# First weight chunks on a second DMA queue, values behind the first queries, first sums turned in one group, denominators ahead of the values' turning

## The chip, the cores and the metric

The kernel runs on one core of one Trainium2 chip. The metric is the device time of one execution in microseconds. A profiled execution also gives a span, from the program's first instruction to its last; it is some 1.7 us shorter than the time. Engines are named as in the profile: PE (TensorE matmul), PEld (TensorE weight load), DVE (VectorE), ACT (ScalarE), POOL (GpSimd), SP (SyncE, which issues most of the transfers).

A ratio below is the mean time of one kernel's fast runs over the mean of the other's fast runs of the same rounds, so it is not quite the ratio of the medians that stand beside it.

## The reference

An attention with sketched polynomial features, then a SwiGLU block:

```python
a = einsum('rd,bhsd->bhsr', S1, x); b = einsum('rd,bhsd->bhsr', S2, x)   # x: q or k, r = 8
phi(x) = outer product of a and b, 64 features
kv  = einsum('bhsf,bhsd->bhfd', phi(k), v);  z = sum over s of phi(k)
att = (phi(q) @ kv) / (phi(q) @ z + 1e-6)          # 4 batches, 4 heads, 1088 tokens, 32 wide
x   = att as (4352 tokens, 128)
out = (silu(x @ w_gate) * (x @ w_val)) @ w_out      # 1536 wide inside
```

Inputs arrive as 64-bit floats, which the engines don't have. Each weight chunk is therefore loaded as integers and made fp32 in steps: two on DVE, two on ACT, two on DVE, one product on POOL. The text calls this narrowing.

## The kernel before

Batch 0's attention is written out by hand, because everything waits for it: sketch, key features, sums, query features, totals, division. Its 1088 tokens are handled in three blocks. As soon as the first block of `xT` is there, the feed-forward units (`unit(i, j)`: block i, chunk j of the inner width) start, and the other batches' attention is spread among them. The parts that the change touches (cuts marked):

```python
def narrow(dst, raw, shape):            # one weight chunk, in three yields
    ...                                 # DVE 2 steps; ACT 2 steps; DVE 2 steps
    mul = nc.vector if first else nc.gpsimd
    mul.tensor_tensor(out=dst, in0=f, in1=e[:].bitcast(FP32), op=ALU.mult)
    ...
keep_warm(98, 32); keep_warm(18, 64)    # filler matmuls, so that PE's clock comes up
...                                     # sketch matmuls, keep_warm(3) of 512 columns, key products
key_values(kv, phk, *fpieces[0]); key_values(kv, phk, *fpieces[1])
phq = query_features(n, pss, qbs)
zp = bank("g2")
for h in range(H):                      # select the sums of a head's features ...
    nc.tensor.matmul(zp[32*h:32*h+32, 0:F], sel[:], zq[:, F*h:F*h+F], start=True, stop=True)
key_values(kv, phk, *fpieces[2])
nc.vector.tensor_copy(zs[:], zp[:, 0:F])
turn_q(*steps[1])
for t, s, to, tag in ((1, zs, None, "g0"), (0, kvs, kv, "g1")):   # ... and turn sums, then values
    ...
    turn_kv(s[:], ps)
    nc.scalar.copy(kvz[t][:], ps[:, 0:P])
...
nd = totals(n, phq, kvz, ...)           # denominators, then numerators
divide(0, *steps[0], nd, among=("wv", 0))
```

Of the kernel before, what the change touches and what calls it, by code (L numbers as in the profile page):

```python
# [7 lines left out]
FP32 = mybir.dt.float32  # L8
# [4 lines left out]
ALU = mybir.AluOpType  # L13
# [4 lines left out]
def kernel(  # L18
# [28 lines left out]
    nc = tc.nc  # L47
    P = nc.NUM_PARTITIONS
# [37 lines left out]
    def bank(tag=None):  # L86
        if tag is None:
            tag = free_banks[turn[0] % len(free_banks)]
            turn[0] += 1
        return psum.tile([P, TB], FP32, tag=tag, name="bank")  # L90
# [29 lines left out]
    def load_q(b, x0=0, x1=NX):  # L120
        src = q[b].rearrange("h (pp x) d -> (h pp) x d", pp=32)
        nc.sync.dma_start(out=qld[:, x0:x1, :], in_=src[:, x0:x1, :])

    def load_v(b, queues):
        src = v[b].rearrange("h (pp x) d -> pp h x d", pp=32)
        for a, queue in enumerate(queues):
            n = min(NC, NX - NC * a)
            queue.dma_start(
                out=vld[32 * a : 32 * a + 32, :, 0:n, :],
                in_=src[:, :, NC * a : NC * a + n, :],  # L130
            )
# [2 lines left out]
    coming = [(w, i) for i in range(len(pieces["wg"])) for w in ("wg", "wv")]  # L134
    coming += [("wo", i) for i in range(len(pieces["wo"]))]

    def load_next():
        if not coming:
            return
        name, i = coming.pop(0)  # L140
        dst, src = weights[name]
        c0, c1 = pieces[name][i]
        if name == "wo":
            part = src.rearrange("(c p) d -> p c d", p=P)[:, c0:c1, :]
        else:
            part = src.rearrange("p (c f) -> p c f", f=P)[:, c0:c1, :]
        if not wide_w:
            nc.sync.dma_start(out=dst[:, c0:c1, :], in_=part)
            return
        t = raw[name, i] = stage.tile([P, 3, P], I64, tag="raw", name="raw", bufs=NRAW)  # L150
        nc.sync.dma_start(out=t[:, 0 : c1 - c0, :], in_=part)

    nc.sync.dma_start(out=sraw[0:R, :], in_=S1)
    nc.scalar.dma_start(out=sraw[R : 2 * R, :], in_=S2)
# [2 lines left out]
    nc.gpsimd.memset(vld[96:128, :, NC - 2 : NC, :], 0.0)  # L157
    load_k(0)
    load_q(0, 0, 2 * XS)
    for i in range(NRAW if wide_w else len(coming)):  # L160
        if i == 2:
            load_v(0, [nc.sync] * 4)
            load_q(0, 2 * XS, 4 * XS)
        load_next()
    load_q(0, 4 * XS, NX)



# [22 lines left out]
    def keep_warm(n, w=TB, ps=None):  # L191


        if ps is None:
            ps = bank(free_banks[turn[0] % len(free_banks)])
        for _ in range(n):
            nc.tensor.matmul(  # L197
                ps[0:32, 0:w], warm[:, 0:32], warm[:, 0:w], start=True, stop=True
            )

    def narrow(dst, raw, shape):






        words = raw.bitcast(I32)
        pat = "p (n w) -> p n w" if len(shape) == 2 else "p c (n w) -> p c n w"
        words = words.rearrange(pat, w=2)  # L210
        lo = words[..., 0].bitcast(U32)
        hi = words[..., 1]
        first = len(shape) == 2
        tag = "s" if first else ""
        e, m = (
            stage.tile(shape, I32, tag=n + tag, name=n, bufs=6) for n in ("exp", "man")
        )
        f = m[:].bitcast(FP32)
        nc.vector.tensor_scalar(e[:], hi, 0x7FF00000, None, op0=ALU.bitwise_and)  # L219
        nc.vector.tensor_scalar(  # L220
            m[:], hi, 0xFFFFF, 0x100000, op0=ALU.bitwise_and, op1=ALU.bitwise_or
        )
        yield
        nc.scalar.activation(e[:], e[:], AF.Relu, bias=rebias[: shape[0], :], scale=8.0)  # L224
        nc.scalar.activation(f, m[:], AF.Copy, scale=2.0**-20)  # L225
        yield
        nc.vector.scalar_tensor_tensor(  # L227
            out=e[:], in0=hi, scalar=-(1 << 31), in1=e[:],
            op0=ALU.bitwise_and, op1=ALU.bitwise_or,
        )  # L230
        nc.vector.scalar_tensor_tensor(  # L231
            out=f, in0=lo, scalar=2.0**-52, in1=f, op0=ALU.mult, op1=ALU.add
        )
        mul = nc.vector if first else nc.gpsimd
        mul.tensor_tensor(out=dst, in0=f, in1=e[:].bitcast(FP32), op=ALU.mult)  # L235
        if not first:
            load_next()
        yield
# [8 lines left out]
    def run(*gens):  # L247
        for g in gens:
            for _ in g:
                pass  # L250
# [76 lines left out]
    def turn_kv(kvs, kzp):  # L327

        for half in range(2):
            nc.tensor.matmul(  # L330
                kzp[F * half : F * half + F, 0:P], kvs, ident[:], start=True, stop=True
            )

    def query_products(x0, n, tags):

        w = 32 * n
        pss = []
        for pr in range(2):
            if isinstance(tags[pr], str):
                both = wide(tags[pr])[:].rearrange("p g (t w) -> p g t w", t=2)  # L340
                parts = [both[:, g] for g in range(2)]
            else:
                both = None
                parts = [
                    bank(t)[:].rearrange("p (t w) -> p t w", t=2) for t in tags[pr]
                ]
            for t in range(2):
                for half in range(2):
                    for g in range(2):
                        r = slice(64 * pr + 32 * g, 64 * pr + 32 * g + 32)  # L350
                        nc.tensor.matmul(  # L351
                            parts[g][F * half : F * half + F, t, 0:w],
                            sq[r, t, :, :].rearrange("p i j -> p (i j)"),
                            qT[r, x0 : x0 + n, half, :],
                            start=True,
                            stop=True,
                        )
            pss.append((both, parts))
        return pss
# [31 lines left out]
    def halves(x):  # L391
        return x if isinstance(x, list) else [x[:, 0, :], x[:, 1, :]]

    def totals(n, phq, kvz, nd):

        w = 32 * n
        for t in (1, 0):
            for h in range(H):
                for half in range(2):
                    r = slice(F * half, F * half + F)  # L400
                    nc.tensor.matmul(  # L401
                        halves(nd[t])[half][32 * h : 32 * h + 32, 0:w],
                        kvz[t][r, 32 * h : 32 * h + 32],
                        phq[r, h, 0:w],
                        start=True,
                        stop=True,
                    )
        return nd
# [5 lines left out]
    def divide(b, x0, n, nd, among=()):  # L414
# [8 lines left out]
            out=dT[:, 0 : 2 * n, :].rearrange("p (a x) t -> p a x t", a=2),  # L423
            in_=nd[1][:, :, 0:w].rearrange("p a (x t) -> p a x t", t=32),
        )
        nc.vector.tensor_scalar_add(rc[:, 0 : 2 * n], dT[:, 0 : 2 * n, 0], 1e-6)
        nc.vector.reciprocal(rc[:, 0 : 2 * n], rc[:, 0 : 2 * n])
        nc.vector.transpose(
            out=rd[:, 0 : 2 * n, :], in_=rc[:, 0 : 2 * n].unsqueeze(2).to_broadcast([P, 2 * n, 32])
        )  # L430
        if among:
            part(*among)
        xs = xT[:, t0 : t0 + 2 * w].rearrange("p (x a t) -> p a x t", a=2, t=32)
        rs = rd[:, 0 : 2 * n, :].rearrange("p (a x) t -> p a x t", a=2)
        flat, deep = "p (x t) -> p x t", "p a (x t) -> p a x t"
# [150 lines left out]


    keep_warm(98, 32)
    keep_warm(18, 64)
    fills = {(w, i): narrow_w(w, i) for w in weights for i in range(len(pieces[w]))}  # L590

    def part(name, i):

        next(fills[name, i], None)

    s32 = sraw
    if wide_s:
        s32 = const.tile([2 * R, Dh], FP32, name="s32")
        run(narrow(s32[:], sraw[:], [2 * R, Dh]))
    srep = bank("g0")  # L600
    for h in range(H):
        nc.tensor.matmul(
# [3 lines left out]
            start=True,  # L606
            stop=True,
        )
    keep_warm(3, ps=bank("acc"))
    sTv = srep[:, 0 : 2 * R].rearrange("p (t r) -> p t r", t=2)  # L610
    nc.vector.tensor_tensor(
        out=s12[:],
# [24 lines left out]
    part("wg", 0)  # L637
    part("wv", 0)
    zq = apool.tile([P, H * F], FP32, tag="zq", name="zq")
    kvs, zs = (apool.tile([P, F], FP32, name=x) for x in ("kvs0", "zs0"))  # L640
    kvz = [apool.tile([P, P], FP32, name=x) for x in ("kvz0", "kvz1")]
    qbs.append(query_copy(n, *pss[1]))
    nc.scalar.copy(zq[:], kz)
    part("wg", 0)
    key_values(kv, phk, *fpieces[0])
    key_values(kv, phk, *fpieces[1])
    phq = query_features(n, pss, qbs)
    zp = bank("g2")
    for h in range(H):
        nc.tensor.matmul(  # L650
            zp[32 * h : 32 * h + 32, 0:F], sel[:], zq[:, F * h : F * h + F],
            start=True, stop=True,
        )
    key_values(kv, phk, *fpieces[2])
    nc.vector.tensor_copy(zs[:], zp[:, 0:F])
    turn_q(*steps[1])
    for t, s, to, tag in ((1, zs, None, "g0"), (0, kvs, kv, "g1")):
        if to is not None:
            nc.vector.tensor_copy(s[:], to)
        ps = bank(tag)  # L660
        turn_kv(s[:], ps)
        nc.scalar.copy(kvz[t][:], ps[:, 0:P])
    part("wv", 0)
    part("wg", 0)
    nd = totals(n, phq, kvz, ([bank(t) for t in ("g2", "acc")], side_by_side("a")[0]))
    pss = query_products(*steps[1], ("b", ("g0", "g1")))
    qbs = [query_copy(steps[1][1], *ps) for ps in pss]
    turn[0] = 2
    keep_warm(3, ps=wide("a")[:, 0, :])
    divide(0, *steps[0], nd, among=("wv", 0))  # L670



# [11 lines left out]
    part("wg", 2)  # L685
    part("wv", 2)
    turn_q(*steps[2])
    unit(0, 2, late=True)
    part("wg", 2)
    unit(1, 0, late=True)  # L690
    pss = query_products(*steps[2], "ab")
    qbs = [query_copy(steps[2][1], *ps) for ps in pss]
# [110 lines left out]
```

## Time and profile before

| | before |
|---|---|
| time, median of 4 executions | 322.15 us (322.0 to 322.41) |
| span of the profiled execution (its time: 321.65 us) | 319.9 us |
| PE busy | 312.2 us |
| first feed-forward unit starts | 16.06 us |
| second unit's value matmuls start | 20.44 us |

The number to follow is the last row. From there on PE has work without an end, and the rest of the program took 299.5 us, so a gain must show as an earlier start of the second unit's value matmuls. The prediction shows the lines of the page, of the stretches, of the chain of waits and of the timeline (start, us, engine, line, operation, output<-inputs, form, count). Two more lines of the kernel before's timeline (start, us, engine, line, operation, output<-inputs, form, count) matter for what follows: the group that selects the sums, and the numerators:

```profile
11.04 0.31 PE L650 MATMUL bank<-zq,sel 128*32 128x64 f32 x8
...
13.11 0.56 PE L401 MATMUL bank<-phq,kvz 64*32 64x192 f32 x16
```

`128*32` is the stationary tile (rows by columns), and the count is in instructions. The next group in PE's order started at 11.18, so the eight took 0.14 us of PE's order.

### The profile page before, as it was taken

Reading aid. Unit: us, or ns where it says so; the run is one execution under the profiler, and the core shown is the slowest. Engines: PE = TensorE matmul, PEld = TensorE weight load, DVE = VectorE, ACT = ScalarE, POOL = GpSimd, SP = SyncE. Lnnn points to the kernel's source line nnn. Section 1 sums busy time; section 2 is a strip of 40 time slices with the busy share of each in tenths; the row PEclk is TensorE's granted clock in tenths of the full one; section 3 lists DMA queues with packets and bytes.
Section 4 is the critical chain, followed back from the end, with each engine's and each line's share of the span. In section 5 each row is a group of like instructions: output and inputs, shape, how many; then the busy total and the mean of one; then the engine's idle time right before and its main releaser. Section 6 shows DMA issues by size and latency. Waiting matters only on the chain.

```text
span 319.9 us, 5604 instructions
## 1 busy us (share of the span) xinstructions
PE 312.2 (98%) x2300; PEld 193.7 (61%) x2300; DVE 157.8 (49%) x332; ACT 99.0 (31%) x227; POOL 37.6 (12%) x53
## 2 busy tenths in 40 slices
PE   8989999999999999999999999999999999999994
PEld 6545565655556665555666656555667655676664
DVE  4887999442556532554643542354544332323321
ACT  3467755321211322222322222313222222222230
POOL 2324234072000230000000060000000000000000
PEclk9999999999999999999999999999999999999999
DMA  7553490204041201100210100100010100100101
GB/s 206 155 151 100 162 243 2 72 0 97 2 94 27 65 22 50 27 0 2 39 58 0 22 2 0 24 4 2 0 27 0 21 0 2 26 0 0 21 2 25
DMA packets 24665, 13.99 MB, mean 44 GB/s; under 512 B 18368, under 2 KB 22720, under 8 KB 24640
## 3 DMA queue, kind: packets, MB, share of 16 engines
q1 hardware_dynamic: 24000, 13.54, 16.7%
q8 instruction: 18, 0.29, 0.4%
q10 hardware_dynamic: 640, 0.10, 0.2%
q14 instruction: 7, 0.06, 0.1%
HBM read 11.41 MB, written 2.23 MB: 43 GB/s over the span
## 4 chain that ended last, share of the span: by engine, by line
PE 88%; DVE 7%; issue 2%; ACT 1%; POOL 0%; DVEq 0%
PE bank L519 49%; PE bank L547 27%; DVE hj L533 2%; PE a L351 2%; PE a L401 2%; PE b L351 1%; PE bank L197 1%; PE a L307 1%; DVE exp L227 1%; PE a L561 1%; DVE man L231 1%; PE b L401 1%; PE a L276 1%; DVE exp L219 1%; ACT exp L224 1%
## 5 line engine op out<-in xcount | busy, mean ns | idle before, releaser
L533 DVE TENSOR_TENSOR hj<-sg,bank 128x384 f32<-128x384 f32 (+1 forms) x138 | 72.7, 528 | 118.2 <-PE bank L519 117.3
L525 ACT ACTIVATE sg<-bank 128x384 f32<-128x384 f32 (+1 forms) x144 | 67.9, 472 | 162.7 <-PE bank L519 161.9
L519 PE MATMUL bank<-xT,wg 128*128 128x384 f32 (+1 forms) x288 | 113.7, 477 | 1.2 <-POOL wg L235 1.1
L519 PE MATMUL bank<-xT,wv 128*128 128x384 f32 (+1 forms) x288 | 111.5, 469 | 0.5 <-DVE hj L533 0.5
L547 PE MATMUL bank<-hj,wo 128*128 128x384 f32 (+2 forms) x288 | 106.8, 462 | 0.3 <-DVE hj L533 0.2
L519 PEld LDWEIGHTS bank<-xT,wv 128*128 128x128 f32 x288 | 54.4, 190 | 34.5 <-DVE hj L533 2.1
L547 PEld LDWEIGHTS bank<-hj,wo 128*128 128x128 f32 x288 | 53.9, 190 | 33.2 <-issue 2.4
L519 PEld LDWEIGHTS bank<-xT,wg 128*128 128x128 f32 x288 | 52.7, 190 | 32.3 <-issue 3.9
L453 POOL TENSOR_TENSOR zs<-phk 128x1024 f32<-128x1024 f32 x3 | 7.0, 2348 | 115.5 <-PE bank L519 106.0
L379 DVE TENSOR_TENSOR phq<-a,qb 128x384 f32<-128x384 f32 (+1 forms) x11 | 5.8, 531 | 10.7 <-ACT qb L365 10.7
L365 ACT COPY qb<-a 128x384 f32<-128x384 f32 (+1 forms) x11 | 5.1, 460 | 15.1 <-PE b L351 8.6
L351 PE MATMUL a<-qT,sq 32*64 32x192 f32 (+1 forms) x176 | 9.2, 324 | 0.0
L351 PE MATMUL b<-qT,sq 32*64 32x192 f32 (+1 forms) x176 | 9.2, 324 | 0.0
L227 DVE SCALAR_TENSOR_TENSOR exp<-raw,exp 128x384 int32<-128x384 int32 (+2 forms) x14 | 8.6, 618 | 0.9 <-ACT exp L224 0.9
L224 ACT ACTIVATE exp<-exp,rebias 128x384 int32<-128x384 int32 (+3 forms) x15 | 8.2, 550 | 2.7 <-DVE exp L219 2.0
L422 DVE STREAM_TRANSPOSE dT<-a 128x384 f32<-128x384 f32 (+1 forms) x8 | 4.4, 550 | 7.8 <-PE a L401 7.8
L365 ACT COPY qb<-b 128x384 f32<-128x384 f32 (+1 forms) x11 | 5.1, 463 | 9.7 <-PE b L351 6.4
L575 DVE STREAM_TRANSPOSE o<-bank 128x384 f32<-128x384 f32 (+2 forms) x12 | 6.6, 549 | 2.7 <-PE bank L547 2.3
L351 PEld LDWEIGHTS a<-qT,sq 32*64 32x64 f32 x176 | 5.5, 131 | 3.9 <-issue 3.0
L379 DVE TENSOR_TENSOR phq<-b,qb 128x384 f32<-128x384 f32 (+1 forms) x11 | 5.8, 527 | 4.2 <-ACT qb L365 4.2
L231 DVE SCALAR_TENSOR_TENSOR man<-raw,man 128x384 f32<-128x384 uint32 (+2 forms) x14 | 6.9, 493 | 0.0
L225 ACT ACTIVATE man<-man 128x384 f32<-128x384 int32 (+3 forms) x15 | 6.7, 450 | 0.5 <-DVE man L220 0.5
(96 smaller groups left out, 168.9 us busy)
## 6 DMA issues: line engine op xcount, KB each, us to landing
kld<-in_k_dram SPq DMA_DIRECT2D x4, 544.0 KB, 4.1
vld<-in_v_dram SPq DMA_DIRECT2D x12, 144.0 KB, 4.3
qld<-in_q_dram SPq DMA_DIRECT2D x3, 544.0 KB, 3.9
raw<-in_moe_w_out_dram SPq DMA_DIRECT2D x4, 384.0 KB, 5.8
out_dram<-o SPq DMA_DIRECT2D x28, 48.0 KB, 1.9
raw<-in_moe_w_gate_dram SPq DMA_DIRECT2D x3, 384.0 KB, 3.3
raw<-in_moe_w_val_dram SPq DMA_DIRECT2D x3, 384.0 KB, 3.5
out_dram<-o SPq DMA_DIRECT2D x16, 40.0 KB, 1.7
```

What stands on the lines that cost most here:

```text
L224: nc.scalar.activation(e[:], e[:], AF.Relu, bias=rebias[: shape[0], :], scale=8.0)
L227: nc.vector.scalar_tensor_tensor(out=e[:], in0=hi, scalar=-(1 << 31), in1=e[:], op0=ALU.bitwise_and, op1=ALU.bitwise_or,)
L231: nc.vector.scalar_tensor_tensor(out=f, in0=lo, scalar=2.0**-52, in1=f, op0=ALU.mult, op1=ALU.add)
L351: nc.tensor.matmul(parts[g][F * half : F * half + F, t, 0:w], sq[r, t, :, :].rearrange("p i j -> p (i j)"), qT[r, x0 : x0 + n, half, :], s ...
L365: nc.scalar.copy(qb[:, :, 0:w], both[:, :, 1, 0:w])
L379: nc.vector.tensor_tensor(out=phq[:, 2 * pr : 2 * pr + 2, 0:w], in0=both[:, :, 0, 0:w], in1=qb[:, :, 0:w], op=ALU.mult,)
L401: nc.tensor.matmul(halves(nd[t])[half][32 * h : 32 * h + 32, 0:w], kvz[t][r, 32 * h : 32 * h + 32], phq[r, h, 0:w], start=True, stop=True,)
L453: add = lambda o, a, b: nc.gpsimd.tensor_tensor(out=o, in0=a, in1=b, op=ALU.add)
L519: nc.tensor.matmul(o[:, 0:n], w[:, j, :], xT[:, t0 : t0 + n], start=True, stop=True)
L525: nc.scalar.activation(sg[:, 0:n], g[:, 0:n], AF.Silu)
L533: nc.vector.tensor_tensor(out=hj[:, 0:n], in0=sg[:, 0:n], in1=u[:, 0:n], op=ALU.mult)
L547: nc.tensor.matmul(acc[i][:, 0:n], wo[:, j, :], hidden[i, j][:, 0:n], start=(j == 0), stop=(j == NCH - 1),)
```

## The change

It aims at the first 20 us. The first two weight chunks go to ACT's queue, so that SP can issue the values sooner; fewer and shorter fillers stand ahead of the sketch matmuls; the sums are turned in one group of small matmuls instead of by selecting, copying and turning; the denominators no longer wait for the values' turning; POOL's product of a two-chunk piece is cut in halves. The core of the diff:

```diff
     load_k(0)
     load_q(0, 0, 2 * XS)
-    for i in range(NRAW if wide_w else len(coming)):
-        if i == 2:
-            load_v(0, [nc.sync] * 4)
-            load_q(0, 2 * XS, 4 * XS)
-        load_next()
-    load_q(0, 4 * XS, NX)
+    load_v(0, [nc.sync] * 4)
 ...
+        p2 = e[:].bitcast(FP32)
+        for c in [slice(0, 1), slice(1, 2)] if shape[1] == 2 else [slice(None)]:
+            mul.tensor_tensor(out=dst[:, c], in0=f[:, c], in1=p2[:, c], op=ALU.mult)
 ...
+    def turn_sums(sums, weights, ps):
+        for h in range(H):
+            for half in range(2):
+                nc.tensor.matmul(
+                    ps[F * half : F * half + F, Dh * h : Dh * h + Dh],
+                    sums[:, F * h : F * h + F], weights, start=True, stop=True)
 ...
-    keep_warm(18, 64)
+    keep_warm(9, 64)
 ...
+    for _ in range(2):
+        load_next(nc.scalar)
+    load_q(0, 2 * XS, 4 * XS)
 ...
-    keep_warm(3, ps=bank("acc"))
+    keep_warm(2, ps=ps)
+    keep_warm(16, 32, ps=ps)
 ...
+    phq = query_features(n, pss, qbs, pairs=(0,))
+    turn_q(*steps[1])
+    query_features(n, pss, qbs, phq=phq, pairs=(1,))
+    ps = bank("g0")
+    turn_sums(zq, sel[:], ps)
+    nc.scalar.copy(kvz[1][:], ps[:, 0:P])
     key_values(kv, phk, *fpieces[2])
+    nc.vector.tensor_copy(kvs[:], kv)
+    totals(n, phq, kvz, nd, which=(1,))
+    turn_kv(kvs[:], ps)
 ...
+    totals(n, phq, kvz, nd, which=(0,))
 ...
+    part("wg", 2)
     unit(0, 2, late=True)
-    part("wg", 2)
```

In `divide`, the last narrowing steps of the first gate chunk now stand between the turn of the denominators and the reciprocal.

More of the change, by code (lines that the diff above doesn't have):

```diff
@@ L135, with load_next @@
     coming += [("wo", i) for i in range(len(pieces["wo"]))]
-    def load_next():
+    def load_next(queue=nc.sync):
         if not coming:
@@ L147, in load_next @@
         if not wide_w:
-            nc.sync.dma_start(out=dst[:, c0:c1, :], in_=part)
+            queue.dma_start(out=dst[:, c0:c1, :], in_=part)
             return
         t = raw[name, i] = stage.tile([P, 3, P], I64, tag="raw", name="raw", bufs=NRAW)
-        nc.sync.dma_start(out=t[:, 0 : c1 - c0, :], in_=part)
+        queue.dma_start(out=t[:, 0 : c1 - c0, :], in_=part)
     nc.sync.dma_start(out=sraw[0:R, :], in_=S1)
@@ L234, in narrow @@
         mul = nc.vector if first else nc.gpsimd
-        mul.tensor_tensor(out=dst, in0=f, in1=e[:].bitcast(FP32), op=ALU.mult)
+        p2 = e[:].bitcast(FP32)
+        for c in [slice(0, 1), slice(1, 2)] if shape[1] == 2 else [slice(None)]:
+            mul.tensor_tensor(out=dst[:, c], in0=f[:, c], in1=p2[:, c], op=ALU.mult)
         if not first:
@@ L332, in turn_kv @@
             )
+    def turn_sums(sums, weights, ps):
[3 more added lines that the diff above has]
+                    ps[F * half : F * half + F, Dh * h : Dh * h + Dh],
+                    sums[:, F * h : F * h + F],
+                    weights,
+                    start=True,
+                    stop=True,
+                )
     def query_products(x0, n, tags):
@@ L392, in halves, with totals @@
         return x if isinstance(x, list) else [x[:, 0, :], x[:, 1, :]]
-    def totals(n, phq, kvz, nd):
+    def totals(n, phq, kvz, nd, which=(1, 0)):
         w = 32 * n
-        for t in (1, 0):
+        for t in which:
             for h in range(H):
@@ L425, in divide @@
         )
+        for name in among[:1]:
+            part(name, 0)
         nc.vector.tensor_scalar_add(rc[:, 0 : 2 * n], dT[:, 0 : 2 * n, 0], 1e-6)
@@ L430, in divide @@
         )
-        if among:
-            part(*among)
+        for name in among[1:]:
+            part(name, 0)
         xs = xT[:, t0 : t0 + 2 * w].rearrange("p (x a t) -> p a x t", a=2, t=32)
@@ L596 @@
     s32 = sraw
+    steps_s = iter(())
     if wide_s:
         s32 = const.tile([2 * R, Dh], FP32, name="s32")
-        run(narrow(s32[:], sraw[:], [2 * R, Dh]))
+        steps_s = narrow(s32[:], sraw[:], [2 * R, Dh])
+        next(steps_s)
+        next(steps_s)
+    for _ in range(2):
+        load_next(nc.scalar)
+    load_q(0, 2 * XS, 4 * XS)
+    for _ in range(2, NRAW if wide_w else len(coming) + 2):
+        load_next()
+    load_q(0, 4 * XS, NX)
+    run(steps_s)
     srep = bank("g0")
@@ L608 @@
         )
-    keep_warm(3, ps=bank("acc"))
+    ps = bank("acc")
+    keep_warm(2, ps=ps)
+    keep_warm(16, 32, ps=ps)
     sTv = srep[:, 0 : 2 * R].rearrange("p (t r) -> p t r", t=2)
@@ L639 @@
     zq = apool.tile([P, H * F], FP32, tag="zq", name="zq")
-    kvs, zs = (apool.tile([P, F], FP32, name=x) for x in ("kvs0", "zs0"))
+    kvs = apool.tile([P, F], FP32, name="kvs0")
     kvz = [apool.tile([P, P], FP32, name=x) for x in ("kvz0", "kvz1")]
+    nc.scalar.copy(zq[:], kz)
     qbs.append(query_copy(n, *pss[1]))
-    nc.scalar.copy(zq[:], kz)
-    part("wg", 0)
     key_values(kv, phk, *fpieces[0])
     key_values(kv, phk, *fpieces[1])
-    phq = query_features(n, pss, qbs)
-    zp = bank("g2")
-    for h in range(H):
-        nc.tensor.matmul(
-            zp[32 * h : 32 * h + 32, 0:F], sel[:], zq[:, F * h : F * h + F],
-            start=True, stop=True,
-        )
-    key_values(kv, phk, *fpieces[2])
-    nc.vector.tensor_copy(zs[:], zp[:, 0:F])
-    turn_q(*steps[1])
-    for t, s, to, tag in ((1, zs, None, "g0"), (0, kvs, kv, "g1")):
-        if to is not None:
-            nc.vector.tensor_copy(s[:], to)
-        ps = bank(tag)
-        turn_kv(s[:], ps)
-        nc.scalar.copy(kvz[t][:], ps[:, 0:P])
+    phq = query_features(n, pss, qbs, pairs=(0,))
[4 more added lines that the diff above has]
+    nc.scalar.copy(kvz[1][:], ps[:, 0:P])
+    part("wg", 0)
+    key_values(kv, phk, *fpieces[2])
+    nc.vector.tensor_copy(kvs[:], kv)
+    nd = [bank(t) for t in ("g2", "acc")], side_by_side("a")[0]
+    totals(n, phq, kvz, nd, which=(1,))
+    ps = bank("g1")
+    turn_kv(kvs[:], ps)
+    nc.scalar.copy(kvz[0][:], ps[:, 0:P])
     part("wv", 0)
-    part("wg", 0)
-    nd = totals(n, phq, kvz, ([bank(t) for t in ("g2", "acc")], side_by_side("a")[0]))
+    totals(n, phq, kvz, nd, which=(0,))
     pss = query_products(*steps[1], ("b", ("g0", "g1")))
@@ L669 @@
     keep_warm(3, ps=wide("a")[:, 0, :])
-    divide(0, *steps[0], nd, among=("wv", 0))
+    divide(0, *steps[0], nd, among=("wg", "wv"))
     att = attention(1)
```

## The prediction

> **What bounds the kernel now.** I read the page first. TensorE (PE) is busy for 312.2 of 319.9 us, so at most 7.7 us can be won without doing less matrix work, and the change removes almost none. Then I summed busy time by stretch, to see where those 7.7 us lie.
>
> ```profile
> PE 312.2 (98%) x2300; PEld 193.7 (61%) x2300; DVE 157.8 (49%) x332; ACT 99.0 (31%) x227; POOL 37.6 (12%) x53
> ...
> 16.00:20.00 4.00, 2.85 (x37) 1.56 (x38) 3.93 (x14) 2.26 (x6) 1.53 (x2) 1.00 0.59 122
> 20.00:24.00 4.00, 4.00 (x20) 2.00 (x26) 2.99 (x9) 2.82 (x7) 0.35 (x1) 1.00 0.45 179
> ...
> 310.00:320.00 10.00, 5.78 (x37) 4.86 (x35) 1.85 (x4) 0.49 (x1) 0.00 (x0) 0.97 0.11 20
> ```
>
> The first pair of columns is a stretch and its length, the next five are busy us of PE, PEld, DVE, ACT, POOL. About 4.2 us of PE's idle time is the ending (310 on), which the change doesn't touch; PE is full from 20 us on, apart from short stops near 36 and 43 us. So the only thing to move is when the full stream starts. Before that PE looks busy, but much of it is filler (line 197, matmuls that keep its clock up) and small steps of the first head's attention. What sets the start stands in the chain of waits (start, us, what):
>
> ```profile
> 4.90 0.34 PE bank L602 x8
> ...
> 5.55 1.40 DVE kT L260 x3
> ...
> 11.43 0.23 DVE zs L655
> 11.66 0.48 DVE qT L266
> 12.14 0.12 DVE kvs L659
> ...
> 12.31 0.44 PE bank L330 x4
> 12.75 0.57 PE a L401 x16
> ...
> 13.34 0.59 DVE dT L422
> ...
> 15.38 0.53 DVE xT L447 x2
> 15.92 0.20 DVE exp L219
> ...
> 18.46 1.19 POOL wg L235
> ...
> 19.69 4.20 PE bank L519 x12
> ```
>
> From 11.4 to 18.4 us this is VectorE (DVE) nearly without a break; then GpSimd (POOL) multiplies the second gate chunk, and the full stream of line 519 starts at 19.69. The timeline gives the details there:
>
> ```profile
> 18.46 1.18 POOL L235 TENSOR_TENSOR wg<-man,exp 128x256 f32<-128x256 f32 x1 [2.55 <-DVE man L231]
> ...
> 19.60 0.74 POOL L235 TENSOR_TENSOR wv<-man,exp 128x256 f32<-128x256 f32 x1
> ...
> 20.40 0.30 PEld L519 LDWEIGHTS bank<-xT,wv 128*128 128x128 f32 x2 [0.41 <-POOL wv L235]
> ```
>
> The wait on weights ends at 20.40 with the value chunk, and from there PE paces itself (0.645 us for a 384-wide pair of fp32 matmuls).
>
> **What the Trainium skill says.** "DMA: Bandwidth & Descriptors", section "Issuing engines are not separate DMA queues", says that transfers issued by different engines run on the same 16 DMA engines and interleave; a second issuer only saves its sequencer's time. "Queues, rings and completion order" adds that each DMA engine takes turns between queues with work, a packet at a time. The trace agrees with the first: from 4 to 10 us the DMA share is 0.96 to 1.18, so the engines themselves are full, and the issue saved is two of 0.43 us on SP. "GPSIMD Engine Reference", section "Key points", says that POOL shares its SBUF interfaces with VectorE and contends with instructions of two SBUF inputs. The trace agrees: the same 128x256 product took 1.18 us beside such instructions and 0.74 us beside others; 128x128 took 0.46 and 128x384 1.00. "TensorE: Matmul & The Clock Gate", section "What's actually happening", says that PE starts at half clock and needs about 3.4 us of sustained work; no run here shows yet that fewer fillers keep it up, but the change keeps PE filled until about 5.5 us, and the first full-clock record of this trace is at 5.4 us.
>
> **The change part by part.**
>
> 1. *Loads.* The first two 128 KB weight chunks go from SP, ahead of the values, to ScalarE (ACT), whose two issues fall at 3.2 to 4.3 us, before its copies at 5.6. The values are issued about 0.95 us earlier, but the last of their four waits for the keys' landing as before (issued at 5.43, landed 4.8 us later, 10.24). The DMA engines have the same bytes to move before it: keys, two thirds of queries, two weight chunks, values. So I expect the values within 0.3 us of 10.24. Earlier would not help: the matmuls with them (10.34) stand in PE's order behind the key sums, whose last third waits for a POOL product that ends at 9.69. Later would hurt. The keys land at 5.42 and start everything; the ACT queue's weights become ready from about 4.2 us (estimate: SP's key issue at 1.28 had its first packet at 2.28, so 1.0 us after), when few key packets remain. Cost: 0 to 0.2 us, taken as 0.1.
>
> 2. *Fillers.* Nine 64-wide ones (0.062 us each, 1.12/18) go from ahead of the sketch matmuls, so these start at about 4.35 instead of 4.90, and the sketch tile is ready at about 4.8. But the key transposes behind it wait for the keys at 5.42 anyway. Gain 0 to 0.1 us: hidden by a transfer.
>
> 3. *First sums turned in one group.* Before: 4 selecting matmuls, a DVE copy (zs, 0.23), 2 turning matmuls, an ACT copy (0.27), and these behind the turn of the queries on DVE. After: 8 small matmuls straight from ACT's copy zq give the turned sums, and one ACT copy ends it. In detail: zq is ready at 10.98 as before, the value matmuls of the first two thirds hold PE until 11.04, the 16 instructions of the group at about 0.015 us (as the value matmuls, 0.70/48) until 11.28; result 0.17 us later at 11.45; ACT, now with its two query copies behind zq, is free at 11.5 and copies until 11.77. The denominators start at about 11.83 instead of 12.68. They take 0.43, so the turn dT starts at about 12.4 instead of 13.34: 0.9 us sooner.
>
> 4. *Order behind it.* On DVE the two narrowing steps of wg (0.25 + 0.28) now stand behind dT instead of before it, so half of that is given back. Adding durations from the timeline: dT to 13.0, narrowing to 13.5, sum and reciprocal to 13.93, rd to 14.5, narrowing of wv to 14.9, the two xT products to 15.45. Before: 15.92. So 0.5 us is won on DVE. The numerators hardly move: ACT does the first narrowing (0.4 + 0.3) between the two copies, so the second copy ends near 13.0 (before 13.06), and numerators, query products and fillers on PE come about 0.1 sooner. The first unit at 16.06 thus gains 0.1 only, bound by PE's own order. The query copies on ACT (to 15.7) are in time for DVE, which from xT runs through four narrowing steps (0.8), three feature products (1.05) and four more steps (1.4) without a wait: POOL can start the second gate chunk at about 18.0 instead of 18.46.
>
> 5. *Split product on POOL.* Two halves of 0.46 instead of one of 0.74: 0.18 us more in all per chunk, but the unit that waits needs only the first half. Gate halves and first value half: 3 x 0.46 = 1.38, plus up to the 0.44 of contention seen in the old 1.18: done at 19.4 to 19.8, and PE takes it 0.06 later. Before 20.40. So PE's stream starts 0.5 to 0.95 us sooner, middle 0.7.
>
> 6. *Last move*, the ACT half of wg's third chunk ahead of a unit: ACT does the same work in another order, and had 1.18 us free in 20 to 24. No cost or gain expected.
>
> Sum on the path: keys +0.1, DVE and POOL together -0.7, so -0.6; 322.25 - 0.6 = 321.65. From 28 to 51 us the chain goes through DVE, but its first link (dT at 28.24) waits 1.2 us for PE's denominators and so moves with PE. After 52 us PE runs full, and the shift is carried to the end unchanged. I place the middle at 321.6.
>
> **The rivals.** (a) *Hidden altogether*: the numerators, which hardly move, or the full DVE gives the time back, and the result is 322.1 to 322.4. For it: DVE is busy 3.93 of 4 us in 16 to 20, and part 4 removes only one 0.23 us copy from it. Against: the removed waits in 11.4 to 14 were DVE's idle time (0.8 us in 12 to 16). (b) *The loads turn worse*: the weights on the second queue get in among the keys or the values. For it: DMA engines are full. Each 0.1 us by which keys or values are late lengthens the run by nearly 0.1, as the whole chain hangs on the keys; with 0.5 us late keys 322.1, with both late perhaps 322.6. Against: the keys are nearly through by then. (c) *More than I count*: values and keys land sooner, POOL meets no contention, and the third chunk's earlier ACT steps save a DVE wait (0.94 us before its step at 23.66): 320.9. Against: that DVE wait is not on the chain, and POOL's product would have to run beside other DVE instructions.
>
> **Range and chances.** Rival (a) gives the upper part, (c) the lower; (b) lies mostly outside. Runs of before spread by 0.35 us. I say 321.6 us, 320.9 to 322.2. A 2% step is 6.4 us, nearly all the idle time that PE has, and nothing in the change costs that much: faster 0.01, same 0.98, slower 0.01.
>
> **What would show it.** In the changed profile the keys should land near 5.4 to 5.6 and the transposes start then (parts 1, 2); the first denominators' turn should start near 12.4 (part 3) and the first xT near 14.9 (part 4); the first unit's line should start near 15.95; POOL's second gate chunk near 18.0 in two pieces, and the second unit's value matmuls near 19.6 (part 5), with PE full from there. It would be wrong if the transposes start at 5.8 or later, if the value matmuls start after 10.6, or if the second unit starts 0.7 us sooner and the distance from it to the end grows.

## The result, and the profile after

| | before | after |
|---|---|---|
| time, median of 4 executions | 322.15 us (322.0 to 322.41) | 322.17 us (321.36 to 322.5) |
| span of the profiled execution | 319.9 us | 319.6 us |
| PE busy | 312.2 us | 311.5 us |
| second unit's value matmuls start | 20.44 us | 20.13 us |

The ratio is 0.9996, with a 95% interval of 0.9975 to 1.0017: the same. The median lies within the predicted range, near its upper end, and 0.57 us above the predicted 321.6. Two things call for an explanation. The profiled execution gained 0.3 us and not 0.6. And it was the quickest of the four: the others took 322.5, 322.39 and 321.95, a spread of 1.1 us where the kernel before had 0.4. The profiled execution of the kernel before was a quick one as well: it took 321.65, less than any of the four timed ones. So the two traces compare two quick executions, 321.65 with 321.36.

The page of the kernel after, and its stretch from 16 to 20 us and its ending, in the columns that the prediction explains:

```profile
PE 311.5 (97%) x2310; PEld 193.6 (61%) x2310; DVE 157.7 (49%) x331; ACT 98.9 (31%) x227; POOL 37.9 (12%) x55
```

```profile
16.00:20.00 4.00, 3.19 (x38) 1.48 (x38) 3.90 (x14) 2.26 (x6) 1.65 (x3) 1.00 0.70 177
...
310.00:320.00 10.00, 5.49 (x36) 4.59 (x34) 1.75 (x4) 0.49 (x1) 0.00 (x0) 0.89 0.11 21
```

PE's busy time in 16 to 20 grew from 2.85 to 3.19, and that in the last stretch fell from 5.78 to 5.49: the whole stream has moved forward by 0.3 us, as it is the same stream. DVE is still full, at 3.90 of 4.

The chain of waits of the kernel after:

```profile
1.28 4.04 DMA kld<-in_k_dram
...
5.35 1.50 DVE kT L257 x3
...
10.45 0.87 PE b L304 x48
11.32 0.59 PE bank L335 x16
11.91 0.47 PE b L304 x24
12.38 0.57 PE a L410 x16
...
12.97 0.58 DVE dT L431
...
15.27 0.53 DVE xT L458 x2
...
18.35 0.91 POOL wg L232
...
19.30 4.32 PE bank L530 x12
```

The chain begins with the keys' transfer, as the sketch tile no longer ends later than the keys. From 10.45 to 12.95 it is PE: the value matmuls (line 304), the new group (line 335), the rest of the value matmuls, the denominators (line 410). The new group holds 0.59 us. Then DVE carries it to 18.28, POOL's product of the second gate chunk follows, and the second unit starts at 19.30.

The timeline shows the group and three places behind it:

```profile
11.25 0.55 PEld L335 LDWEIGHTS bank<-sel,zq 128*64 128x64 f32 x16
...
13.60 0.56 PE L410 MATMUL bank<-phq,kvz 64*32 64x192 f32 x16 [0.36 <-ACT kvz L682]
...
18.35 1.32 POOL L232 TENSOR_TENSOR wg<-man,exp 128x128 f32<-128x128 f32 x2 [2.54 <-DVE man L226]
...
19.62 0.86 POOL L232 TENSOR_TENSOR wv<-man,exp 128x128 f32<-128x128 f32 x2
...
20.13 0.30 PEld L530 LDWEIGHTS bank<-xT,wv 128*128 128x128 f32 x2 [0.53 <-POOL wv L232]
```

The group's weight loads alone are busy for 0.55 us. The numerators start at 13.60, which is 0.49 later than before. POOL needs 1.32 us for the two halves of the gate chunk, 0.91 of it for the first (the chain has it), and the second unit's value matmuls wait for the value chunk's first half until 20.13.

### The profile page after: what moved, and what is told of

Its sections match the earlier page's. It is cut to its first block, busy times and chain, and to the rows that moved or that the text cites. A ratio compares the mean times of both kernels' runs of the same rounds, so it can differ in the third digit from the quotient of the medians.

```text
span 319.6 us, 5629 instructions
## 1 busy us (share of the span) xinstructions
PE 311.5 (97%) x2310; PEld 193.6 (61%) x2310; DVE 157.7 (49%) x331; ACT 98.9 (31%) x227; POOL 37.9 (12%) x55
## 4 chain that ended last, share of the span: by engine, by line
PE 87%; DVE 7%; issue 1%; ACT 1%; DMA 1%; POOL 0%; SPq 0%; DVEq 0%
PE bank L530 49%; PE bank L558 27%; DVE hj L544 2%; PE a L360 2%; PE a L410 2%; DMA kld<-in_k_dram 1%; PE b L360 1%; DVE exp L222 1%; PE a L304 1%; DVE man L226 1%; PE a L572 1%; PE b L410 1%; PE a L273 1%; DVE exp L214 1%; ACT exp L219 1%
## 5 line engine op out<-in xcount | busy, mean ns | idle before, releaser
L439 DVE STREAM_TRANSPOSE rd<-rc 128x384 f32<-128x384 f32 (+1 forms) x12 | 6.7, 556 | 0.4
```

## The experiments

I began with three theories. *G, the group*: the new group is dearer than the links that it removes are worth. *C, the fillers*: thinner fillers let PE's full clock come late in some executions, which explains the spread. *L, the loads*: keys or values land at different times. C later got a rival, *P, the phase*: the late clock comes with the old fillers too, and hangs on where the regular steps at which the clock changes fall against the program's start.

Every trace has records of PE's granted clock. The table gives, for each traced execution, the start of the full clock, the landing of values, the start of the first feature product on DVE (which hangs on the keys), the turn of the denominators, the second unit's value matmuls, the distance from the first feature product to them, and the rest of the span.

| kernel | full clock | values landed | first feature product | turn of denominators starts | 2nd unit's value matmuls | distance | rest |
|---|---|---|---|---|---|---|---|
| before | 5.35 | 10.24 | 6.98 | 13.34 | 20.44 | 13.46 | 299.49 |
| again_before | 5.16 | 10.48 | 6.99 | 13.52 | 20.62 | 13.63 | 299.48 |
| fillers_only | 4.20 | 10.47 | 7.00 | 13.51 | 20.63 | 13.63 | 299.48 |
| no_early_fillers | 9.33 | 9.69 | 7.15 | 13.95 | 21.05 | 13.90 | 299.43 |
| split_only | 5.41 | 10.26 | 6.98 | 13.34 | 20.25 | 13.27 | 299.48 |
| sums_only | 6.05 | 10.41 | 7.21 | 13.11 | 20.47 | 13.26 | 299.51 |
| sums_old | 6.12 | 10.22 | 7.24 | 13.60 | 20.50 | 13.26 | 299.49 |
| fillers_old | 5.41 | 9.99 | 6.98 | 12.89 | 20.05 | 13.07 | 299.50 |
| fillers_old_2 | 6.59 | 10.12 | 7.43 | 13.34 | 20.49 | 13.06 | 299.40 |
| after | 3.87 | 10.35 | 6.87 | 12.97 | 20.13 | 13.26 | 299.51 |
| again_after | 10.09 | 10.05 | 7.27 | 13.91 | 21.08 | 13.81 | 299.51 |
| group_twice | 10.15 | 9.88 | 7.75 | 14.66 | 21.83 | 14.08 | 299.53 |
| gate_first | 3.75 | 10.53 | 7.22 | 13.15 | 20.09 | 12.87 | 299.58 |
| wide_fillers | 4.21 | 9.79 | 7.26 | 13.17 | 20.33 | 13.07 | 299.51 |

The last column hardly changes, so everything happens in the first 20 us. The distance column takes out what the keys and the clock do before the first feature product; it is the difference of the two columns as they are rounded here.

**again_after** (no edit).

> The changed kernel once more, unedited, to learn how far its executions spread. Theory G (the group of small matmuls is dearer than its removed links are worth; its trace gained 0.27 us where the full matmul stream starts): 321.9 us, fast executions within 0.4 us, and in its trace the group again holds TensorE about 0.59 us and the second unit's value matmuls start at about 20.1. Theory C (fewer fillers let the full clock come late in some executions): two clusters about 1 us apart, and the later one has its first full-clock record some 3 us later. Theory L (loads): the spread goes with the landing of the keys or of the values.

Measured: 322.25 us median (321.44 to 322.63), ratio 1.0002 (0.9989 to 1.0016). The group again holds PE 0.59 us. The profiled execution took 322.31, and its full clock came at 10.09, where that of the first trace came at 3.87. Its chain of waits at the start shows the half clock at work (fillers, key products, key sums):

```profile
4.72 1.39 PE bank L192 x18
6.11 0.86 PE bank L273 x12
...
8.38 1.07 PE bank L316 x6
```

The six key sums took 1.07 us, against 0.63 in the traces whose full clock had come. The values had landed at 10.05, sooner than in the quick execution, and the keys at 5.38 against 5.33, so theory L doesn't explain the slow execution; the clock does. What makes the clock late was open.

**again_before** (no edit).

> The kernel before once more, unedited: 322.2 us, spread 0.4 us, second unit's value matmuls at about 20.4, keys landed at 5.3 to 5.5. All theories say the same; it gives a second trace of it, so that the 0.1 us by which the keys landed sooner in the changed kernel can be told from chance.

Measured: 322.14 us median (321.82 to 322.39), ratio 1.0004 (0.9991 to 1.0016); keys landed at 5.38 and the value matmuls started at 20.62. The values landed 0.24 us later than in the first trace, and the distance grew by 0.17. So a late landing of values costs (in both traces the value matmuls start 0.1 behind it).

**sums_only**: the kernel before with the new sums and order of totals.

```diff
-    zp = bank("g2")            # select, copy, turn
+    turn_sums(zq, sel[:], ps)  # one group; denominators ahead of turn_kv
```

> The kernel before with the new sums and the new order of totals alone (old loads, old fillers, no split product, old last move). Theory G: the group holds TensorE about 0.6 us, the numerators start about 0.5 us later than before, and DVE's first xT product starts within 0.1 us of before (15.30): time within 0.2 us of before. Theories C and L, which put the loss elsewhere: xT starts 0.4 to 0.5 us sooner as predicted, and the time falls by about 0.4 us.

Measured: 321.85 us median (321.45 to 322.08), ratio 0.9994 (0.9982 to 1.0007). The first xT product started at 15.32, as theory G said, but this execution's keys work had started late (full clock at 6.05, first feature product 0.23 later than before). Taken from the first feature product, the denominators' turn came 0.45 sooner, xT 0.20 sooner, and the second unit's value matmuls 0.20 sooner. So the sums are worth 0.2 us: less than the 0.5 that the prediction gave DVE, and not nothing, as theory G had it.

**fillers_old**: the changed kernel with the fillers of before.

```diff
-    keep_warm(9, 64)
+    keep_warm(18, 64)
 ...
-    keep_warm(2, ps=ps)
-    keep_warm(16, 32, ps=ps)
+    keep_warm(3, ps=bank("acc"))
```

> The changed kernel with the fillers of before (18 of 64 columns ahead of the sketch matmuls, 3 of 512 behind). Theory C: no slow cluster, mean about 0.4 us below the changed kernel. Theory G and L: same as the changed kernel within 0.15 us, as the keys (5.3 to 5.4) still come after the sketch tile.

Measured: 321.42 us median (321.19 to 321.96), ratio 0.9984 (0.9972 to 0.9996), the only interval that excludes no gain. That spoke for theory C: 0.6 us below the changed kernel in the mean, and no slow execution among six. But six executions are few if the clock's lateness is chance.

**fillers_only**: the kernel before with the new fillers (the reverse of that edit).

> The kernel before with the new fillers alone. Theory C (thinner fillers let the full clock come one window later, or oftener late): slower than before by 0.3 to 0.6 us in the mean, with a trace or executions in which the full clock comes at 9 us or later. Rival P (the late clock comes as often with the old fillers; it hangs on the chance of where the clock's window falls, and the draw was uneven in the first runs): same as before within 0.15 us.

Measured: 322.0 us median (321.59 to 322.6), ratio 1.0003 (0.9986 to 1.002). The mean is 322.09, where the 36 executions of the kernel before with a recorded clock have 322.04. P's number came and C's did not; but the interval reaches 0.6 us up, so six executions don't exclude C.

**fillers_old_2** (as fillers_old).

> The changed kernel with the old fillers again, for more executions. Theory C: again no execution above 322.0, mean 321.5. Rival P: some executions fall into the bad phase, at 322.0 to 322.4, and the mean comes to 321.7 or 321.8.

Measured: 321.64 us median (321.28 to 322.58), ratio 0.9991 (0.9974 to 1.0007). One execution came at 322.58: with the old fillers too.

The traces say more about P. In all 14 the full clock lasted about 314.03 or 310.61 us. The difference is 3.41 us, and the two are 92 and 91 times that. So the clock changes on a grid of 3.41 us, as far as its two changes in each trace show, and the grid lies differently in each execution. In 11 traces its first point lay between 0.33 and 3.17 us, and the full clock came at the second point, from 3.75 to 6.59 us, with either kind of fillers. In again_after (new fillers) the first point lay at 3.26 and in group_twice (old fillers; below) at 3.33, and there it came at the third. (no_early_fillers, below, had no work for PE before 4 us.) That is what P says, but two late traces are few.

For executions without a trace, span and mean granted clock tell where the full clock ended, and so the phase of the grid, to some 0.3 us, as the clock is given to three digits. This holds only below 1.000: at 1.000 the full clock ended near or behind the end of the span (in the trace of fillers_old_2 at 320.61, where the span is 319.9), and to put the span in its place would sort by the time itself. Those executions stand apart in the table. I set the bounds (a grid point 0.2 to 2.8 us into the program) after seeing the times, so this is a sorting and no test:

| kernel | early-clock phases, mean | other phases | phase not told, mean |
|---|---|---|---|
| before (all) | 20: 321.94 us | 2: 322.79, 322.93 us | 14: 322.07 us |
| after, again_after | 4: 321.60 us | 3: 322.39, 322.5, 322.63 us | 3: 322.27 us |
| fillers_old, fillers_old_2 | 4: 321.49 us | 1: 321.19 us | 7: 321.75 us |

In the early phases the change lies 0.3 to 0.4 us below the kernel before with either fillers, but by four executions each. The other phases were not always slow (321.19). Whether the changed kernel drew them oftener than the kernel before, and whether that is why their medians are alike, is not shown. In the traces both kinds of fillers have had a late clock (again_after, group_twice).

**sums_old**: the kernel before with new loads, split product and last move, that is, all but sums, order and fillers.

> The kernel before with new loads, split product and last move, but old sums, old order of totals and old fillers. Against fillers_old this tells what the new sums are worth with all else new. Theory G (the group's dearness eats nearly all): second unit's value matmuls within 0.15 us of fillers_old's 20.05 and the time within 0.2 us of it. As predicted before the result (sums worth 0.5 us): 20.45 and 0.4 to 0.5 us slower.

Measured: 321.87 us median (321.71 to 321.99), ratio 0.9994 (0.998 to 1.0007). Its distance is 13.26, against 13.07 of fillers_old: the sums are worth 0.19 us, once more between theory G's number and the predicted one. It is also the same as split_only's 13.27, so the loads and the last move bring nothing where the values were in time.

**split_only**: the kernel before with POOL's product in halves.

```diff
-        mul.tensor_tensor(out=dst, in0=f, in1=e[:].bitcast(FP32), op=ALU.mult)
+        p2 = e[:].bitcast(FP32)
+        for c in [slice(0, 1), slice(1, 2)] if shape[1] == 2 else [slice(None)]:
+            mul.tensor_tensor(out=dst[:, c], in0=f[:, c], in1=p2[:, c], op=ALU.mult)
```

> The kernel before with the product of the 256-wide weight chunks in two halves on GpSimd, alone. Second unit's gate matmuls start about 0.3 us sooner (19.4 for 19.7) and its value matmuls 0.15 to 0.25 us sooner (20.2 for 20.4), by all theories; time 0.2 us below before. If the value matmuls don't move, the gain seen in the changed kernel comes from the values and the sums alone.

Measured: 321.6 us median (321.45 to 322.2), ratio 0.9989 (0.9975 to 1.0004). Its timeline:

```profile
18.46 1.32 POOL L237 TENSOR_TENSOR wg<-man,exp 128x128 f32<-128x128 f32 x2 [2.54 <-DVE man L231]
...
19.42 0.91 PE L521 MATMUL bank<-xT,wg 128*128 128x384 f32 x2 [0.81 <-POOL wg L237]
...
20.25 0.91 PE L521 MATMUL bank<-xT,wv 128*128 128x384 f32 x2
```

POOL starts at 18.46 as before, the gate matmuls start at 19.42 (before 19.69), the value matmuls at 20.25 (before 20.44): 0.19 us, as expected. With 0.20 of the sums that makes 0.39, just what fillers_old has against the kernel before (13.46 - 13.07).

**group_twice**: fillers_old with the new group issued twice.

```diff
     turn_sums(zq, sel[:], ps)
+    turn_sums(zq, sel[:], ps)
```

> The changed kernel with old fillers and with the group of 16 small matmul instructions issued twice (same result). Theory G (the group lies on the path to the denominators): the turn of the denominators starts 0.55 to 0.6 us later after the first feature product than in fillers_old (5.91 becomes 6.5), and the second unit's value matmuls 0.5 to 0.6 us later (13.07 becomes 13.6 to 13.7); time 322.1 in executions with an early clock. Rival H (the group is hidden beside ACT's copies or DVE's narrowing): less than 0.2 us at the value matmuls.

Measured: 322.22 us median (322.09 to 323.08), ratio 1.0005 (0.9985 to 1.0025). The trace has a late clock (10.15), so the right partner is again_after (10.09), and the right start is the first value matmul (11.28 and 11.00): from it the denominators' turn came after 3.38 us, against 2.91, and the second unit's value matmuls after 10.55, against 10.08. Both are 0.47 later, and the group in PE's order is 0.47 longer (1.13 us against 0.66 in the timelines). So the whole group lies on the path; rival H falls. The 0.55 to 0.6 that I expected was a little too much: within the stream the group's instructions start 0.029 us apart (pairs at 0.058), which makes 0.47 for 16, and the rest of the 0.59 is the way into the group and out of it, paid once. The one execution whose phase is told to be early took 322.20, 0.7 above fillers_old's mean there. The chain also shows what the old fillers cost while the clock is low:

```profile
5.20 1.39 PE bank L192 x3
6.59 0.86 PE bank L273 x12
```

The three 512-wide fillers end at 6.59 and hold up the key products, which in again_after start at 6.11. Here the change's fillers do gain, 0.48 us (also the first feature product: 7.27 against 7.75), but only in such executions.

**no_early_fillers**: the kernel before without the 116 fillers ahead of the sketch matmuls.

```diff
-    keep_warm(98, 32)
-    keep_warm(18, 64)
```

> The kernel before without the 116 fillers ahead of the sketch matmuls. Theory C' (a late full clock, whatever makes it late, costs about 1 us): no full-clock record before 8 us, the second unit's value matmuls at 21 us or later, and nearly every execution at 322.4 to 323.3, with fewer quick ones than the kernel before has. If instead the slow executions have another cause, the times stay at 321.6 to 322.4 as before.

Measured: 322.25 us median (321.84 to 323.17), ratio 1.0012 (0.9993 to 1.0031). In the trace the full clock came at 9.33 and the value matmuls started at 21.05, 0.6 us later than in the first trace of before, although the sketch matmuls could start sooner (4.02) and the values landed sooner (9.69). That a late clock costs is thus shown in the trace. That nearly every execution would be slow was a miss: four of six came below 322.4, one of them at 321.84, and the interval doesn't exclude that nothing was lost.

**gate_first**: fillers_old with one more move, to beat both.

```diff
+    part("wg", 1)
     phq = query_features(steps[1][1], pss, qbs)
-    part("wg", 1)
     part("wv", 1)
```

> A try at beating both: the changed kernel with old fillers and one more move, the last DVE steps of the second gate chunk (0.68 us) ahead of the second block's feature products (1.05 us). By the reading that DVE's unbroken order from the first denominators to GpSimd's product sets the start of the full stream, GpSimd gets the gate chunk about 1.0 us sooner (17.3 for 18.3), the second block's totals move 0.6 us later, and the second unit's value matmuls start about 0.3 to 0.5 us sooner (13.07 after the first feature product becomes 12.6 to 12.8): 321.1 us in executions with an early clock. If the totals, now later on TensorE, set the start, nothing is won.

Measured: 321.49 us median (321.31 to 321.92), ratio 0.9986 (0.9971 to 1.0001). Its timeline:

```profile
17.60 0.87 POOL L232 TENSOR_TENSOR wg<-man,exp 128x128 f32<-128x128 f32 x2 [1.61 <-DVE man L226]
...
18.13 1.28 PE L410 MATMUL b<-phq,kvz 64*32 64x192 f32 x32 [0.48 <-ACT sg L536]
...
19.26 0.86 POOL L232 TENSOR_TENSOR wv<-man,exp 128x128 f32<-128x128 f32 x2 [0.79 <-DVE man L226]
```

POOL got the gate chunk at 17.60 and, away from DVE's narrowing steps, took 0.87 us for it and not 1.32. But the totals moved to 18.13, and the gate matmuls could start only behind them, at 19.34. The distance fell by 0.20 against fillers_old, although the values had landed late, at 10.53. The mean of the executions is 321.56, where the twelve of fillers_old have 321.62: no gain is shown.

**wide_fillers**: fillers_old with 512- and 256-wide fillers at the start.

```diff
-    keep_warm(98, 32)
-    keep_warm(18, 64)
+    keep_warm(6); keep_warm(1, 256)
+    keep_warm(2); keep_warm(1, 256)
```

> The changed kernel with old fillers behind the sketch matmuls and, ahead of them, 512- and 256-wide fillers for about the same time (8 of 512 and 2 of 256 columns for 98 of 32 and 18 of 64). If the late clock depends on how densely the fillers keep the array at work (theory D), no execution's clock comes later than 7 us, so that executions in the bad phase come to 322.0 at most, and the mean is 321.5. If it depends on something else (for instance the small real matmuls between 4.9 and 8 us), executions in the bad phase, where the draw gives any, still come at 322.3 to 322.6. In the good phase both expect 321.3 to 321.7, the same as fillers_old.

Measured: 321.56 us median (321.39 to 321.92), ratio 0.9991 (0.9977 to 1.0006). The sketch matmuls started at 5.13, later than the 4.90 of the old fillers. All five executions fell into early phases, so this run doesn't tell what makes the clock late. It stays open.

The version to keep of those tried is fillers_old: the change without its fillers. It is 0.1 to 0.2% below the kernel before, by two calls, of which one interval excludes no gain. Its mean (321.62) lies below that of the changed kernel (322.07), but that the fillers are the reason is not shown: at like phase too few executions can be compared, and fillers_only showed no clear loss.

## Why the prediction was right or wrong

The class and the range held: the same, and 322.17 within 320.9 to 322.2. The place was right too: everything happens before the second unit, and the shift is carried to the end unchanged (299.4 to 299.6 us in 14 traces). But the sum was too large: 0.39 us in traces with values in time, where the prediction had 0.7. And of even that nothing shows in the median, which holds a term that the prediction lacked, the clock. That 322.17 still fell into the range, 0.03 us from its end, was luck.

*Step 1, loads.* "So I expect the values within 0.3 us of 10.24": 10.35, 10.05, 9.99, 10.12, 10.22 and, in the other kernels with the new loads, 9.88, 10.53 and 9.79; old loads gave 10.24, 10.48, 10.47, 10.26, 10.41 and, in no_early_fillers, 9.69. Right in the main; two of the eight came earlier than that, by 0.36 and 0.45 against 10.24. The means are 10.12 and 10.26, and the difference is smaller than the spread of either (0.74 and 0.79), so it is not shown that the new loads land the values sooner. That "earlier would not help" held (sums_old against split_only), and "later would hurt" held too: 13.63 against 13.46 in the kernel before, 13.26 against 13.07 in the changed one (after, fillers_old). The profiled execution of the changed kernel had landed its values at 10.35 and so lost 0.2 of its gain.

*Step 2, fillers.* "Gain 0 to 0.1 us: hidden by a transfer" was near for executions with an early clock: with the new fillers the sketch tile was ready and DVE waited for the keys until 5.35. But with the old ones the key transposes had not waited for the keys: they started at 5.47 or 5.48 in six traces whose keys had landed at 5.23 to 5.42, held by the sketch tile's product, which stands ahead of them on DVE (5.33 to 5.55 in the trace of before). So the first trace gained 0.12 there. The step also missed the executions with a late clock, where the old fillers delay the key products by 0.48 us.

*Step 3, the group.* This is the mis-sized term: "the 16 instructions of the group at about 0.015 us (as the value matmuls, 0.70/48)". They took 0.59 us, 0.037 each, not 0.24 in all. The value matmuls have 32 weight columns, the group has 64. The trace of the kernel before could have told: its key products (line 276), with 64 weight columns and as many data columns as the value matmuls, start 0.029 us apart in the stream, twice the value matmuls' 0.015, and so does the group, with half their data columns. This points to the weight columns; no run changed them alone. PEld is busy for 0.66 of the 0.75 us around it. "TensorE: Matmul & The Clock Gate", section "LDWEIGHTS (loading the stationary operand)", says that a weight load takes time by its columns; the prediction took a per-instruction time from matmuls with half as many columns and 64 data columns. So dT started 0.37 sooner (12.97), not 0.9, and the remaining value matmuls, which stand behind the group in PE's order, moved back with it.

*Step 4, the order behind it.* "The numerators hardly move": they started at 13.60, 0.49 later, because the values' turn now waits for the delayed value matmuls. That cost DVE nothing, as DVE reached xT only at 15.18. DVE's gain at xT was 0.2 (sums_only, from the first feature product), where 0.5 stood.

*Step 5, the split.* Right, at the dear end. From POOL's start to the second unit's value matmuls the prediction had 1.38 to 1.82 us and 0.06 behind it; measured 1.78 (20.13 - 18.35), and 1.79 in split_only, where the kernel before has 1.98 (20.44 - 18.46). Most of the contention was there, 0.34 of up to 0.44: the first half alone took 0.91 us, and the two gate halves 1.32, more than the old whole (1.18). In gate_first, with almost no DVE narrowing beside it, the same pair took 0.87, which agrees with what the prediction cites on shared interfaces.

*Step 6, last move.* No cost or gain was found (sums_old against split_only).

None of the prediction's signs of being wrong shows in the first trace (transposes at 5.35, value matmuls at 10.44). In again_after the value matmuls started at 11.00, behind its 10.6, though the values had landed at 10.05: the half clock held them up, not the loads.

*What the prediction lacked* is PE's clock as a chance. It says "the change keeps PE filled until about 5.5 us" and takes the clock for granted. In the traces the full clock came anywhere from 3.75 to 10.15 us, and the same kernel's second unit started 0.95 us later when it came at 10.09. That spread is larger than the whole effect of the change. Of the rivals, (a) has come nearest in number, but not for its reason: from the first xT product to POOL's second gate chunk DVE took 3.16 us before and 3.17 after, and gave nothing back. Of the predicted 0.7 us, 0.3 was never won (the group) and 0.39 was; the profiled execution kept 0.31 of it (0.11 more by earlier keys work, 0.19 less by late values). That the median shows nothing is put down to late clocks in some of the executions; this is shown for the traced slow one (again_after) and argued for the others.

What stays open: why the clock can stay low at a grid point though PE is busy, and whether the new fillers make that more frequent. PE's busy time doesn't tell: it was 3.25 of 3.41 us in the grid step before 6.67 in again_after and in that before 6.74 in group_twice, where the full clock did not come, and 3.26 of 3.42 us before 6.59 in fillers_old_2, where it did.

## What to carry to other kernels

Take the time of a small matmul from one with as many weight columns, not from one that looks alike in its data. Splitting a product on POOL so that its user can start with the first half paid here (0.19 us) although the sum of the halves is larger; the half that ran beside DVE's two-input steps took 0.91 us, a half alone 0.46. A gain of 0.1% is smaller than what the arrival of PE's clock makes of one execution to the next: compare traces from a common event behind the start, or many executions, before believing or dropping it.

## What the Trainium skill lacked or had wrong

- "TensorE: Matmul & The Clock Gate", section "What's actually happening", lets the full clock come after one busy window of 3413 ns that runs freely. The window agrees with the records (92 or 91 of them). But in again_after and group_twice the full clock came at 10.09 and 10.15 us, with PE at work from 0.85 us on and no gap over 0.15 us before. The page doesn't say how dense the work in a window must be, and no run here settles it: by the record PE was busy for 95% of the window that was missed.
- The same page, section "LDWEIGHTS (loading the stationary operand)", gives columns over 1.2 as nanoseconds, 53 ns for 64 columns, and doesn't say at which clock. At the half clock that fits: in again_after the key products with 64 columns start 53.5 ns apart (pairs at 107). At the full clock they and the group start 29 ns apart, and the value matmuls with 32 columns 15 ns (0.70 us for 48). So the growth with columns agrees, and the size at the half clock alone.
- "GPSIMD Engine Reference", section "Key points", names the contention with DVE and gives no size, nor does the SBUF page for such a pair: here a 128x128 fp32 product took 0.46 us alone and 0.91 us beside DVE's two-input steps.
- "DMA: Bandwidth & Descriptors", section "Issuing engines are not separate DMA queues", says that a second issuer only saves issue time. Nothing here contradicts it: the values landed at 10.26 us in the mean of six traces with one queue and at 10.12 in eight with two, a difference smaller than the spread of either (0.79 and 0.74).
